# Retention units ahead of the first layer, and a table of powers that goes through memory, in a kernel of retention and two MLPs

## The chip, the cores and the metric

The kernel runs on one core of a Trainium2 chip. The metric is the time of one execution on the device in microseconds (us). The engines are TensorE (PE in the rows, PEld for its weight loads), VectorE (DVE), ScalarE (ACT), GpSimd (POOL) and SyncE (SP), which here issues every DMA.

## What is computed

Retention over 2 batches, 8 heads, 768 positions of 64 features; its output, 1536 tokens of 512 features, goes through two MLPs of width 2048 one after the other.

```
for b in range(nb):                       # blocks of the sequence
    intra = einsum('bhic,bhjc->bhij', qb, kb) * Dmask      # Dmask: lam ** (i - j), below the diagonal
    intra = einsum('bhij,bhjd->bhid', intra, vb)
    inter = einsum('bhid,bhde->bhie', qb * lam_pow, kv_state)
    out[:, :, sl] = intra + inter
    kv_state = lam_block * kv_state + einsum('bhsd,bhse->bhde', kb * rev_pow, vb)
x = out.transpose(0, 2, 1, 3).reshape(1536, 512)
x = square(relu(x @ w_in)) @ w_out        # first MLP (l = 0)
h = x @ w_in2;  out = maximum(0.01 * h, h) @ w_out2        # second MLP (l = 1)
```

The MLP weights arrive as 8-byte floats, which no engine computes with. They are split on the chip into two 4-byte parts, and every product of the MLPs is made of three matmuls: high by high, high by low, low by high.

## The kernel before

**Retention.** There are 12 units, one for each batch and each 128 positions (chunk). For a unit i, `load` fetches k, q and v (256 KB each); `transposes(i)` turns k and q on PE and copies them out on ACT (kT, qT); `scale_q` makes qS on DVE for chunks after the first; `scores(i)` fills two PSUM banks; `mask(i)` multiplies them on DVE with the table of powers DTr into Pm; `state(i)` scales k with kdec on POOL (kd), multiplies it with v on PE, and updates st on DVE with the help of tmp from POOL; `output(i)` is made of matmuls with st and qS (not in the first chunk of a batch) and with Pm and v, and `split` writes its high part on ACT (xhi) and its low part on DVE (xlo). Four units fill a token tile of 512 columns, so there are three token tiles. The last chunk of a batch needs no `state`.

**The table.** On DVE `pw` gets 8 rows of powers, one row for each head in a partition of its own. `table()` spreads them: for each head one DMA of 64 KB, in which every one of the 128 partitions of DTr reads 512 bytes of that row, shifted by one element. `kdec`, which `state` needs, is copied on DVE out of DTr, and LR comes from `rows_of_powers` on PE.

**The MLPs.** `steps` lists l, s, t: two MLPs, four stages of 512 of the 2048 columns, three token tiles; 24 in all. `first` has four groups of 12 matmuls 128x512, each group evacuated as g (high and low part ghi, glo); `second` has four groups of 12, added up in `acc`. So a `first` or a `second` is 48 matmuls, and the MLPs are 24 x 96 = 2304 (the last group is cut into halves of 256 columns). A stage needs four blocks of weights, two of w_in and two of w_out, 1 MB each. `fetch` issues the DMA of a block into one of two buffers `raw`, and `convert` turns it into high and low parts with seven DVE instructions (L104 to L114) and two on ACT.

**The order.** Within `retention` the order on SP and PE is that of the program; on the other engines, and after retention everywhere, a scheduler orders the instructions. PE starts an instruction only after the one ahead of it in its order. The loop over the units fetches a block in every second unit, calls `convert` in every second unit from the fourth on, and from the fifth unit on puts one group of `meanwhile`, the first and second layer of the first step, behind each unit. After the loop the rest of `meanwhile` follows, and then `first` of a step and `second` of the one before it take turns. `warm` is a number of transposes whose results are not used.

Of the kernel before, what the change touches and what calls it, by code (L numbers as in the profile page):

```python
# [19 lines left out]
def tile_retention_then_two_mlps(  # L20
# [28 lines left out]
    ctx.enter_context(nc.allow_non_contiguous_dma(reason="head slices, power table"))  # L49
    xp = ctx.enter_context(tc.tile_pool(name="xp", bufs=1))  # L50
# [41 lines left out]
    def convert():  # L92
        if not fetched:
            return
# [9 lines left out]
        ve.tensor_scalar(out=hf, in0=hf, scalar1=2.0 ** -15, scalar2=122368.0, op0=ALU.max, op1=ALU.min)  # L104
        ve.tensor_scalar(out=hb, in0=hb, scalar1=3, scalar2=0x3FFFFFFF,
                         op0=ALU.logical_shift_left, op1=ALU.bitwise_and)
        ve.scalar_tensor_tensor(out=hb, in0=w_hi, scalar=0xC0000000, in1=hb,  # L107
                                op0=ALU.bitwise_and, op1=ALU.bitwise_or)

        ve.tensor_scalar(out=rb, in0=hb, scalar1=0xFF800000, scalar2=None, op0=ALU.bitwise_and)  # L110
        ve.scalar_tensor_tensor(out=rf, in0=w_lo, scalar=2.0 ** -52, in1=rf, op0=ALU.mult, op1=ALU.mult)
        ve.tensor_tensor(out=hf, in0=hf, in1=rf, op=ALU.add)  # L112
        nc.scalar.copy(hi, hf)  # L113
        ve.tensor_tensor(out=lo, in0=hf, in1=hi, op=ALU.subtract)  # L114
# [13 lines left out]
    def retention(ctx_att, att, meanwhile):  # L128
# [83 lines left out]
        kdec = att.tile([P, NP, 2], F32, name="kdec")  # L212

        def table():

            for h in range(H):
                row = pw[h:h + 1, 1:C + 1]
                dma(DTr[:, h % 2, h // 2, :],
                    bass.AP(tensor=row.tensor, offset=row.offset, ap=[list(row.ap[0]), [1, P], [1, C]]))

        def rows_of_powers():
            ps = bank().rearrange("p (a s) -> p a s", a=NP)
            for p in range(NP):
                nc.tensor.matmul(ps[:, p, :], mine[:, p * P:(p + 1) * P], pw[:, 0:C][:, ::-1], start=True, stop=True)
            return ps

        def transposes(i):
            for name, dst in (("k", kT), ("q", qT)):
# [4 lines left out]
                if i == 0:  # L233
                    warm(3 if name == "k" else 8)
# [26 lines left out]
        def state(n):  # L261
            b, c = units[n]
            if c == NCH - 1:
# [5 lines left out]
                in1=kdec.rearrange("s a (r o) -> s a r o", o=1).to_broadcast([P, NP, 2, D]), op=ALU.mult)  # L269
# [37 lines left out]
        FILL = TT // C  # L307
        table()
        load(0, "v")
        load(2, "kq")  # L310
# [120 lines left out]
    for _ in second(*steps[-1]):  # L431
        pass
# [25 lines left out]
```

## Time and profile before

| | us |
|---|---|
| median of 3 runs | 618.4 (618.04 to 618.56) |
| the profiled execution | 618.69 |
| its span, from the first to the last instruction | 616.9 |
| PE busy | 587.6 |
| DVE busy | 402.0 |
| ACT busy | 250.9 |
| POOL busy | 25.0 |

The span is what the trace shows; 1.8 us of the execution lie around it. The chain of work that ended last is 88% PE, 5% DVE and 3% DMA, so the time is read along PE: how long it works for the MLPs, and what keeps it from doing so. The windows of the trace give busy time, the clock that TensorE was granted (1.00 is 2.4 GHz, 0.50 is 1.2 GHz) and the share of the 16 DMA engines for any stretch.

### The profile page before, as it was taken

How to read it: one execution, taken by the hardware profiler on the slowest of the kernel's cores; microseconds unless marked ns; L12 is line 12 of the kernel's file. 1: busy time of each engine (PE TensorE's matmuls, PEld its weight loads, DVE VectorE, ACT ScalarE, POOL GpSimd, SP SyncE). 2: the span in 40 equal slices, each digit the busy share in tenths (PEclk: the TensorE clock that was granted, in tenths of full speed). 3: DMA queues.
4: the chain of work that ended last, by engine and by line, in shares of the span. 5: the costliest groups of instructions: out<-in, count | busy, mean ns of one | idle time of the engine just before them, and what ended most of it. 6: DMA issues, size and time to landing. Idle time of an engine off the chain costs nothing.

```text
span 616.9 us, 7702 instructions
## 1 busy us (share of the span) xinstructions
PE 587.6 (95%) x3162; PEld 489.5 (79%) x3162; DVE 402.0 (65%) x545; ACT 250.9 (41%) x378; POOL 25.0 (4%) x37
## 2 busy tenths in 40 slices
PE   7088899999999999999999999999999999999997
PEld 6077688888888888888888888888888888888886
DVE  2169999999592939475776977582959453343342
ACT  2034364586654437244636353534333141132120
POOL 1133130000000000000000000000000000000000
PEclk9599799999999999999999999999999999999999
DMA  6799842434421221204040403040210000000112
GB/s 81 84 228 268 212 122 70 163 109 140 133 72 65 70 69 68 69 4 134 0 137 0 127 10 133 5 137 0 69 69 0 1 0 2 0 2 0 69 41 96
DMA packets 57411, 47.16 MB, mean 76 GB/s; under 512 B 38304, under 2 KB 39584, under 8 KB 57376
## 3 DMA queue, kind: packets, MB, share of 16 engines
q1 hardware_dynamic: 57376, 46.67, 27.0%
q8 instruction: 25, 0.41, 0.3%
q14 instruction: 10, 0.08, 0.0%
HBM read 42.99 MB, written 3.15 MB: 75 GB/s over the span
## 4 chain that ended last, share of the span: by engine, by line
PE 88%; DVE 5%; DMA 3%; SPq 2%; ACT 1%; issue 1%; DVEq 0%
PE ps L397 42%; PE ps L362 14%; PE ps L363 14%; PE ps L364 14%; SPq L61 2%; DMA DTr<-pw 2%; DMA raw<-in_moe_w_in 1%; DVE Pm L254 1%; PE ps L249 1%; PE ps L298 1%; PE ps L300 1%; PE ps L273 1%; PE ps L232 0%; DVE hb L107 0%; DVE hb L112 0%
## 5 line engine op out<-in xcount | busy, mean ns | idle before, releaser
L362 PE MATMUL ps<-xhi,whi 128*128 128x512 f32 x384 | 150.8, 393 | 0.0
L363 PE MATMUL ps<-xlo,whi 128*128 128x512 f32 x384 | 150.1, 391 | 0.0
L364 PE MATMUL ps<-xhi,wlo 128*128 128x512 f32 x384 | 150.1, 391 | 0.0
L402 DVE TENSOR_TENSOR acc<-ps,acc 128x512 f32<-128x512 f32 (+1 forms) x73 | 49.7, 681 | 65.0 <-PE ps L397 64.9
L362 PEld LDWEIGHTS ps<-xhi,whi 128*128 128x128 f32 x384 | 72.6, 189 | 15.6 <-issue 0.2
L364 PEld LDWEIGHTS ps<-xhi,wlo 128*128 128x128 f32 x384 | 72.5, 189 | 15.3
L363 PEld LDWEIGHTS ps<-xlo,whi 128*128 128x128 f32 x384 | 72.7, 189 | 15.0
L397 PE MATMUL ps<-wlo,ghi 128*128 128x512 f32 (+1 forms) x196 | 75.4, 385 | 0.0
L397 PE MATMUL ps<-whi,glo 128*128 128x512 f32 (+1 forms) x196 | 75.4, 385 | 0.0
L397 PE MATMUL ps<-whi,ghi 128*128 128x512 f32 (+1 forms) x196 | 75.4, 385 | 0.0
L397 PE MATMUL ps<-ghi,whi 128*128 128x512 f32 x192 | 75.0, 391 | 0.0
L397 PE MATMUL ps<-glo,whi 128*128 128x512 f32 x192 | 74.7, 389 | 0.0
L397 PE MATMUL ps<-ghi,wlo 128*128 128x512 f32 x192 | 74.7, 389 | 0.0
L372 ACT ACTIVATE r<-ps 128x512 f32<-128x512 f32 x48 | 28.7, 598 | 93.0 <-PE ps L364 92.8
L367 ACT ACTIVATE r<-ps 128x512 f32<-128x512 f32 x48 | 28.5, 593 | 64.8 <-PE ps L364 64.8
L373 DVE TENSOR_TENSOR r<-ps,r 128x512 f32<-128x512 f32 x48 | 33.1, 689 | 33.0 <-ACT r L372 33.0
L114 DVE TENSOR_TENSOR wlo<-hb,whi 128x1024 fp32r<-128x1024 f32 x32 | 40.3, 1271 | 21.8 <-ACT whi L113 21.8
L370 DVE TENSOR_TENSOR glo<-r,ghi 128x512 fp32r<-128x512 f32 x48 | 33.4, 698 | 31.9 <-ACT r L369 31.8
L113 ACT CAST whi<-hb 128x1024 fp32r<-128x1024 f32 x32 | 33.1, 1051 | 42.1 <-PE ps L397 29.3
L65 DVE TENSOR_TENSOR glo<-r,ghi 128x512 fp32r<-128x512 f32 x48 | 33.2, 691 | 22.2 <-ACT ghi L64 22.0
L64 ACT CAST ghi<-r 128x512 fp32r<-128x512 f32 x48 | 29.8, 620 | 37.5 <-DVE r L373 37.5
L103 ACT ACTIVATE hb<-raw 128x1024 f32<-128x1024 f32 x32 | 36.7, 1148 | 16.2 <-DMA raw<-in_moe_w_out 6.2
(70 smaller groups left out, 725.5 us busy)
## 6 DMA issues: line engine op xcount, KB each, us to landing
raw<-in_moe_w_in SPq DMA_DIRECT2D x16, 1024.0 KB, 5.4
raw<-in_moe_w_out SPq DMA_DIRECT2D x16, 1024.0 KB, 5.0
k<-in_k SPq DMA_DIRECT2D x12, 256.0 KB, 5.8
q<-in_q SPq DMA_DIRECT2D x12, 256.0 KB, 4.8
v<-in_v SPq DMA_DIRECT2D x12, 256.0 KB, 6.4
out<-acc SPq DMA_DIRECT2D x11, 256.0 KB, 2.0
DTr<-pw SPq DMA_DIRECT2D x8, 64.0 KB, 9.9
out<-acc SPq DMA_DIRECT2D x2, 128.0 KB, 1.7
```

The costliest lines, as they stand in the source:

```text
L64: nc.scalar.copy(hi, src)
L65: nc.vector.tensor_tensor(out=lo, in0=src, in1=hi, op=ALU.subtract)
L103: nc.scalar.activation(hf, w_hi.bitcast(F32), AF.Abs)
L113: nc.scalar.copy(hi, hf)
L114: ve.tensor_tensor(out=lo, in0=hf, in1=hi, op=ALU.subtract)
L362: nc.tensor.matmul(ps, hi_w[:, kk, ms], xhi[t][:, kk], start=kk == 0, stop=False)
L363: nc.tensor.matmul(ps, hi_w[:, kk, ms], xlo[t][:, kk], start=False, stop=False)
L364: nc.tensor.matmul(ps, lo_w[:, kk, ms], xhi[t][:, kk], start=False, stop=kk == KD - 1)
L370: nc.vector.tensor_tensor(out=glo[:, m], in0=r, in1=ghi[:, m], op=ALU.subtract)
L373: nc.vector.tensor_tensor(out=r, in0=ps, in1=r, op=ALU.max)
L397: nc.tensor.matmul(ps, a, b, start=kk == 0 and n == 0, stop=kk == KF - 1 and n == 2)
L402: nc.vector.tensor_tensor(out=a, in0=ps, in1=a, op=ALU.add)
```

## The change

Four things are different, and one follows from them.

- The table: `pw` is stored to memory (`tab`, 8 KB), and two DMAs of 256 KB read it back, one for even heads and one for odd ones, with 512 bytes for each partition and head. The store is ahead of three loads on SP, the two reads behind two of them. `kdec` comes from a transpose of `pw` on PE and a copy on ACT.
- The start: `state(0)` and the transposes of k of unit 2 stand ahead of `mask(0)`, and `output(0)`, the transposes of q of unit 2, `mask(1)` and `scores(2)` stand ahead of the loop; there are fewer `warm`.
- The loop: no group of the MLPs is in it. Only units 0 and 2 fetch a block. `convert` became a generator, so that one unit makes one of the seven DVE instructions of a block (units 5 and 10 make two), 12 in all; these are held in the order of the program.
- The MLPs: for stage 0 of the first MLP the three `first` come in a row, then the `second` of tiles 2, 0 and 1. Tile 2 keeps its g in the space of acc0 and acc1 until its `second` is done. After that `first` and `second` take turns as before. The weights of the following stage are asked for at every sixth piece of that list.
- The rest of `fetch` and `convert` of stage 0 follows behind retention, beside the first layer.

```diff
-    def retention(ctx_att, att, meanwhile):
+    def retention(ctx_att, att):
...
-        kdec = att.tile([P, NP, 2], F32, name="kdec")
+        kdec = att.tile([P, H], F32, name="kdec")
+
+        tab = dram.tile([H, W], F32, name="tab")
 
         def table():
-
-            for h in range(H):
-                row = pw[h:h + 1, 1:C + 1]
-                dma(DTr[:, h % 2, h // 2, :],
-                    bass.AP(tensor=row.tensor, offset=row.offset, ap=[list(row.ap[0]), [1, P], [1, C]]))
+            for par in range(2):
+                row = tab[par:par + 1, 1:C + 1]
+                dma(DTr[:, par], bass.AP(tensor=row.tensor, offset=row.offset, ap=[[1, P], [2 * W, NP], [1, C]]))
+
+        def column_of_powers():
+            ps = bank()[:, 0:H]
+            nc.tensor.transpose(ps, pw[:, 1:C + 1], ident[0:H, 0:H])
+            nc.scalar.copy(kdec, ps)
...
         n_units = len(units)
         FILL = TT // C
+        dma(tab, pw)
+        load(0, "v")
+        load(2, "k")
         table()
-        load(0, "v")
-        load(2, "kq")
+        load(2, "q")
         load(1, "v")
         transposes(0)
         scores(0)
-        lr_psum = rows_of_powers()
-        nc.scalar.copy(LR, lr_psum)
+        column_of_powers()
+        rows_of_powers()
         scale_q(1, transposes(1))
         scores(1)
-        for par in range(2):
-            ve.tensor_copy(kdec[:, :, par], DT[:, par, :, C - 1])
+        state(0)
+        transposes(2, "k")
         mask(0)
-        warm(6)
+        warm(2)
+        output(0)
+        scale_q(2, transposes(2, "q"))
+        mask(1)
+        scores(2)
         for i in range(n_units):
-            if 0 < i < n_units - 2:
-                scale_q(i + 2, transposes(i + 2))
+            if i:
+                if i + 2 < n_units:
+                    scale_q(i + 2, transposes(i + 2))
             if i + 3 < n_units:
                 load(i + 3, "kq")
             if i + 2 < n_units:
                 load(i + 2, "v")
-            if i % 2 == 0:
+            if i in (0, 2):
                 fetch()
-            state(i)
-            output(i)
-            if i == 0:
-                warm(6)
-                scale_q(2, transposes(2))
-            if i + 1 < n_units:
-                mask(i + 1)
-            if i + 2 < n_units:
-                scores(i + 2)
-            if i >= FILL - 1 and i % 2:
-                convert()
-            if i >= FILL:
-                next(meanwhile, None)
-        for _ in meanwhile:
-            pass
+            if i:
+                state(i)
+                output(i)
+                if i + 1 < n_units:
+                    mask(i + 1)
+                if i + 2 < n_units:
+                    scores(i + 2)
+            if i > 1:
+                convert(2 if i % 5 == 0 else 1)
...
     def first(l, s, t):
         hi_w, lo_w = wts[l, s][:2]
-        n = steps.index((l, s, t)) % 2
-        ghi = place[n].tile([P, KF, TT], F32R, tag=f"ghi{n}", name=f"ghi{n}")
-        glo = place[n].tile([P, KF, TT], F32R, tag=f"glo{n}", name=f"glo{n}")
+
+        n = steps.index((l, s, t)) % 2 if l or s else t
+        tags = (f"ghi{n}", f"glo{n}") if n < 2 else ("acc0", "acc1")
+        ghi, glo = (place[n % 2].tile([P, KF, TT], F32R, tag=tag, name=tag) for tag in tags)
...
-            retention(ctx_att, att, chain(first(*steps[0]), second(*steps[0])))
+            retention(ctx_att, att)
     place[1] = ctx.enter_context(tc.tile_pool(name="late", bufs=1, reuse_waits="tile"))
+    line = [first(*steps[0]), first(*steps[1]), first(*steps[2])]
+    line += [second(*steps[2]), second(*steps[0]), second(*steps[1]), first(*steps[3])]
+    for i in range(4, len(steps)):
+        line += [first(*steps[i]), second(*steps[i - 1])]
+    line.append(second(*steps[-1]))
     turn = 0
-    for i, (l, s, t) in enumerate(steps):
-        if t == 0:
-            ls = l * NS + s + 1
-            if ls < 2 * NS:
-                load_w(*divmod(ls, NS))
-        work = first(l, s, t) if i else ()
-        if i > 1:
-            work = chain(work, second(*steps[i - 1]))
+    for i, work in enumerate(line):
+        if i % (2 * NTILE) == 0 and i // (2 * NTILE) + 1 < 2 * NS:
+            load_w(*divmod(i // (2 * NTILE) + 1, NS))
         for _ in work:
             turn += 1
-            if turn % 4 == 1:
+            if turn % 4 == 1 or turn == 2:
                 fetch()
-            elif turn % 4 == 3:
-                convert()
-    for _ in second(*steps[-1]):
-        pass
+            if turn % 4 == 3 or turn == 1:
+                convert(pin=turn < 8)
```

What this does to the order on three engines stands below. A row is an instruction in its place, with what it writes and reads; the line numbers of the changed kernel are higher.

On SP at the start of the program, before: the eight DMAs of the table stand behind the loads of units 0 and 1.

```order
L61 DMA q<-in_q 128x8x64
L61 DMA DTr<-pw 128x1x128 x8
L61 DMA v<-in_v 128x8x64
L61 DMA k<-in_k 128x8x64
L61 DMA q<-in_q 128x8x64
L61 DMA v<-in_v 128x8x64
```

The same place on SP, now:

```order
L62 DMA q<-in_q 128x8x64
L62 DMA tab<-pw 8x256
L62 DMA v<-in_v 128x8x64
L62 DMA k<-in_k 128x8x64
L62 DMA DTr<-tab 128x4x128 x2
L62 DMA q<-in_q 128x8x64
L62 DMA v<-in_v 128x8x64
```

One store and two reads took the place of eight DMAs, and v of unit 0 and k of unit 2 moved ahead of the reads.

On PE in the middle of retention, before, at unit 6: L362 to L364 are the end of a group of the first layer, L232 the transposes, L273 `state`, L300 `output`, L249 `scores`, and then the next group begins.

```order
L362 MATMUL ps<-xhi_297,whi_73 128x512
L363 MATMUL ps<-xlo_298,whi_73 128x512
L364 MATMUL ps<-xhi_297,wlo_74 128x512
L232 MATMUL ps<-ident,k 128x128 x4
L232 MATMUL ps<-ident,q 128x128 x4
L273 MATMUL ps<-v,kd 64x64 x8
L300 MATMUL ps<-Pm,v 64x128 x8
L249 MATMUL ps<-qT,kT 128x128 x8
L362 MATMUL ps<-xhi_297,whi_73 128x512
```

On PE, now, at the one place where retention and first layer meet: the end of `output(11)` (L324, L326) and the first matmuls of the MLPs (L390 to L392).

```order
L324 MATMUL ps<-qS,st_174 64x128 x2
L326 MATMUL ps<-Pm,v 64x128 x2
L324 MATMUL ps<-qS,st_174 64x128 x2
L326 MATMUL ps<-Pm,v 64x128 x2
L390 MATMUL ps<-xhi_287,whi_75 128x512
L391 MATMUL ps<-xlo_288,whi_75 128x512
L392 MATMUL ps<-xhi_287,wlo_76 128x512
```

The groups of 12 that stood between the units moved behind the last unit.

On DVE in retention, before, around units 3 to 5: L104 to L114 are the instructions of a conversion, L254 is `mask`, L242 qS, L285 the update of st, L65 xlo.

```order
L110 TENSOR_SCALAR rb<-hb 128x1024
L65 TENSOR_TENSOR xlo_298<-ps,xhi_297 128x4x128
L254 TENSOR_TENSOR Pm<-ps,DTr 128x512 x2
L111 SCALAR_TENSOR_TENSOR rb<-raw,rb 128x1024
L242 TENSOR_TENSOR qS<-ps,LR 128x512
L285 TENSOR_TENSOR st_169<-ps,tmp 64x4x64 x2
L112 TENSOR_TENSOR hb<-hb,rb 128x1024
L65 TENSOR_TENSOR xlo_298<-ps,xhi_297 128x4x128
L254 TENSOR_TENSOR Pm<-ps,DTr 128x512 x2
L114 TENSOR_TENSOR wlo_74<-hb,whi_73 128x4x256
L104 TENSOR_SCALAR hb<-hb 128x1024
L105 TENSOR_SCALAR hb<-hb 128x1024
```

The same stretch on DVE, now (L280 is `mask`, L268 qS, L311 st, L66 xlo):

```order
L280 TENSOR_TENSOR Pm<-ps,DTr 128x512 x2
L104 TENSOR_SCALAR hb<-hb 128x1024
L268 TENSOR_TENSOR qS<-ps,LR 128x512
L311 TENSOR_TENSOR st_174<-ps,tmp 64x4x64 x2
L66 TENSOR_TENSOR xlo_288<-ps,xhi_287 128x4x128
L280 TENSOR_TENSOR Pm<-ps,DTr 128x512 x2
L105 TENSOR_SCALAR hb<-hb 128x1024
```

Between two masks stands one instruction of a conversion, where there were two to three.

## Rows read from the trace of the kernel before

**Rows 1.** The page's first line, then rows of the timeline of PE and of the chain that ended last (start us, us, what): the first second-layer matmul behind the last retention unit, one whole `second`, the last matmul.

```profile
span 616.9 us, 7702 instructions
...
106.93 0.50 PE L397 MATMUL ps<-ghi,whi 128*128 128x512 f32 x1
...
156.18 10.88 PE ps L397 x48
...
613.01 0.28 PE L397 MATMUL ps<-whi,glo 128*128 128x256 f32 x1
```

**Rows 2.** Windows of the trace: from and to in us, length, then busy us (and instructions) of PE, PEld, DVE, ACT and POOL, granted clock of PE, mean share of the 16 DMA engines, GB/s that they moved.

```profile
12.00:14.00 2.00, 1.27 (x16) 0.91 (x12) 0.00 (x0) 0.00 (x0) 0.00 (x0) 1.00 0.66 25
...
30.00:40.00 10.00, 9.28 (x122) 8.25 (x120) 6.12 (x12) 2.74 (x5) 4.64 (x7) 0.86 1.01 244
40.00:50.00 10.00, 8.62 (x140) 7.48 (x136) 8.29 (x13) 4.43 (x7) 2.84 (x4) 1.00 0.95 242
50.00:60.00 10.00, 7.36 (x101) 6.03 (x100) 9.81 (x15) 5.39 (x8) 4.19 (x4) 1.00 0.98 249
60.00:70.00 10.00, 8.36 (x98) 7.11 (x98) 9.93 (x12) 3.85 (x6) 1.04 (x1) 1.00 0.93 217
...
70.00:75.00 5.00, 4.15 (x21) 3.54 (x22) 4.87 (x9) 1.80 (x4) 0.45 (x1) 0.54 1.09 266
```

**Rows 3.** The timeline of all engines at the start (start us, us, engine, line, operation, and in brackets how long the engine was idle before it and what it waited for): the table's DMAs, PE's last work before the wait, the copy for kdec, the first mask.

```profile
6.54 14.16 SPq L61 DMA_DIRECT2D DTr<-pw  x8
...
12.39 0.87 PE L164 MATMUL ps<-ident 128*128 128x128 f32 x6
...
26.96 0.17 DVE L319 COPY kdec<-DTr 128x4 f32<-128x4 f32 x1 [20.51 <-DMA DTr<-pw]
...
28.19 1.28 DVE L254 TENSOR_TENSOR Pm<-ps,DTr 128x512 f32<-128x512 f32 x2
```

**Rows 4.** The chain that ended last, at its start: the load of lam, and the last piece of pw.

```profile
0.74 1.36 DMA sq<-in_lam
...
6.21 0.25 DVE pw L184
```

**Rows 5.** DMA issues by line: the two half-width stores of the result, with their count, KB of each, and median us from issue to landing.

```profile
out<-acc SPq DMA_DIRECT2D x2, 128.0 KB, 1.7
```

**Rows 6.** The timeline again: `scores` of unit 1, and the first transposes of a unit in the loop, for units 3, 4 and 7.

```profile
11.30 1.16 PE L249 MATMUL ps<-qT,kT 64*128 64x128 f32 x16 [0.73 <-ACT qT L236]
...
36.07 0.66 PE L232 MATMUL ps<-ident,k 128*128 128x128 f32 x4
...
41.60 0.63 PE L232 MATMUL ps<-ident,k 128*128 128x128 f32 x4 [0.99 <-DMA k<-in_k]
...
57.37 0.66 PE L232 MATMUL ps<-ident,k 128*128 128x128 f32 x4
```

**Rows 7.** The timeline of PE: `output` of unit 6, the first chunk of its batch; and one unit where PE never paused: its transposes, `state`, the first matmuls of `output`, `scores`, and what follows them.

```profile
67.31 1.05 PE L300 MATMUL ps<-Pm,v 128*64 128x128 f32 x16
...
85.05 0.60 PE L232 MATMUL ps<-ident,k 128*128 128x128 f32 x4
...
86.02 0.69 PE L273 MATMUL ps<-v,kd 128*64 128x64 f32 x16
86.53 0.39 PE L298 MATMUL ps<-qS,st 128*64 128x128 f32 x4
...
88.38 1.16 PE L249 MATMUL ps<-qT,kT 64*128 64x128 f32 x16
89.47 0.50 PE L362 MATMUL ps<-xhi,whi 128*128 128x512 f32 x1
```

**Rows 8.** The timeline of DVE in retention: qS, st, a conversion's instruction, xlo, mask, and two more of the conversion.

```profile
46.06 0.68 DVE L242 TENSOR_TENSOR qS<-ps,LR 128x512 f32<-128x512 f32 x1
...
46.66 0.86 DVE L285 TENSOR_TENSOR st<-ps,tmp 64x256 f32<-64x256 f32 x2
...
47.55 0.75 DVE L110 TENSOR_SCALAR rb<-hb 128x1024 uint32<-128x1024 uint32 x1
...
48.34 0.69 DVE L65 TENSOR_TENSOR xlo<-ps,xhi 128x512 fp32r<-128x512 f32 x1
...
48.95 1.28 DVE L254 TENSOR_TENSOR Pm<-ps,DTr 128x512 f32<-128x512 f32 x2
50.14 1.21 DVE L111 SCALAR_TENSOR_TENSOR rb<-raw,rb 128x1024 f32<-128x1024 uint32 x1
...
55.89 1.93 DVE L114 TENSOR_TENSOR wlo<-hb,whi 128x1024 fp32r<-128x1024 f32 x1
```

**Rows 9.** The timeline of PE around a pause: `scores` of unit 8 after it, and the matmul that follows.

```profile
70.85 2.08 PE L249 MATMUL ps<-qT,kT 64*128 64x128 f32 x16 [2.49 <-ACT qT L236]
72.86 0.79 PE L362 MATMUL ps<-xhi,whi 128*128 128x512 f32 x1
```

**Rows 10.** The timeline of ACT in the first layer: the first of the three instructions that evacuate a group, the same of the next group, and the two instructions of a conversion.

```profile
127.46 0.59 ACT L367 ACTIVATE r<-ps 128x512 f32<-128x512 f32 x1
...
129.29 0.58 ACT L367 ACTIVATE r<-ps 128x512 f32<-128x512 f32 x1
...
131.80 1.06 ACT L113 CAST whi<-hb 128x1024 fp32r<-128x1024 f32 x1 [0.60 <-DVE hb L112]
...
135.90 1.15 ACT L103 ACTIVATE hb<-raw 128x1024 f32<-128x1024 f32 x1 [1.22 <-DVE glo L370]
```

More of the change, by code (lines that the diff above doesn't have):

```diff
@@ L49, in tile_retention_then_two_mlps @@
     ctx.enter_context(nc.allow_non_contiguous_dma(reason="head slices, power table"))
+    dram = ctx.enter_context(tc.tile_pool(name="dram", bufs=1, space=bass.MemoryType.DRAM))
     xp = ctx.enter_context(tc.tile_pool(name="xp", bufs=1))
@@ L90, in fetch, with converting @@
             fetched.append((r, hi, lo))
-    def convert():
-        if not fetched:
-            return
+    def converting():
         r, hi, lo = fetched.pop(0)
@@ L103, in convert @@
         nc.scalar.activation(hf, w_hi.bitcast(F32), AF.Abs)
[L104 to L112, printed above, removed]
-        nc.scalar.copy(hi, hf)
-        ve.tensor_tensor(out=lo, in0=hf, in1=hi, op=ALU.subtract)
+        yield ve.tensor_scalar(out=hf, in0=hf, scalar1=2.0 ** -15, scalar2=122368.0, op0=ALU.max, op1=ALU.min)
+        yield ve.tensor_scalar(out=hb, in0=hb, scalar1=3, scalar2=0x3FFFFFFF,
+                               op0=ALU.logical_shift_left, op1=ALU.bitwise_and)
+        yield ve.scalar_tensor_tensor(out=hb, in0=w_hi, scalar=0xC0000000, in1=hb,
+                                      op0=ALU.bitwise_and, op1=ALU.bitwise_or)
+        yield ve.tensor_scalar(out=rb, in0=hb, scalar1=0xFF800000, scalar2=None, op0=ALU.bitwise_and)
+        yield ve.scalar_tensor_tensor(out=rf, in0=w_lo, scalar=2.0 ** -52, in1=rf, op0=ALU.mult, op1=ALU.mult)
+        yield ve.tensor_tensor(out=hf, in0=hf, in1=rf, op=ALU.add)
+        nc.scalar.copy(hi, hf)
+        yield ve.tensor_tensor(out=lo, in0=hf, in1=hi, op=ALU.subtract)
+    at_work = []
+    def convert(steps=None, pin=True):
+        done = 0
+        while steps is None or done < steps:
+            if not at_work:
+                if not fetched or (steps is None and done):
+                    return
+                at_work.append(converting())
+            step = next(at_work[0], None)
+            if step is None:
+                at_work.pop()
+                if steps is None:
+                    return
+            else:
+                done += 1
+                if pin:
+                    tc.keep_in_program_order(step)
     wts, todo, fetched = {}, [], []
@@ L224, in rows_of_powers, with transposes @@
                 nc.tensor.matmul(ps[:, p, :], mine[:, p * P:(p + 1) * P], pw[:, 0:C][:, ::-1], start=True, stop=True)
-            return ps
-        def transposes(i):
-            for name, dst in (("k", kT), ("q", qT)):
+            nc.scalar.copy(LR, ps)
+        def transposes(i, names="kq"):
+            for name in names:
+                dst = {"k": kT, "q": qT}[name]
                 ps = bank().rearrange("p (a s) -> p a s", a=NP)
@@ L233, in transposes @@
                 if i == 0:
-                    warm(3 if name == "k" else 8)
+                    warm(3 if name == "k" else 4)
                 dst[i] = tr.tile([P, NP, C], F32, tag=name, name=name + "T")
@@ L268, in state @@
                 out=kd, in0=kn.rearrange("s (a r) d -> s a r d", r=2),
-                in1=kdec.rearrange("s a (r o) -> s a r o", o=1).to_broadcast([P, NP, 2, D]), op=ALU.mult)
+                in1=kdec.rearrange("s (a r o) -> s a r o", r=2, o=1).to_broadcast([P, NP, 2, D]), op=ALU.mult)
             ps = bank()[:, 0:NP * D].rearrange("p (a e) -> p a e", a=NP)
```

## The prediction

> **What bounds the kernel now.** I read the end first. Behind the last retention unit PE works for the MLPs without a pause from 106.93 us to 613.01 + 0.28 = 613.3 us [rows 1]. One `first` or `second` of 48 matmuls takes 10.88 us there, 0.2267 us a matmul. At 106.93 us 72 of the 2304 matmuls were done (the `first` of step 0 and half of its `second`), so the MLPs need 506.4 + 72 x 0.2267 = 522.7 us of PE, and 613.3 - 522.7 = 90.6 us of PE time went to something else. I call that the lead. Nothing in the change touches the 522.7 us or the 3.6 us from 613.3 to the end of the span, so the question is how long the lead becomes.
>
> The start comes second. The last piece of pw is ready at 6.46 us [rows 4], the first mask starts at 28.19 us [rows 3]. In between DVE waits 20.51 us for the table's DMAs; PE has its last work at 12.39 us and waits as well. While the table moves, the DMA engines carry 25 GB/s; with the loads of k, q, v and weights they carry 217 to 249 [rows 2].
>
> Then the stretch from the first mask to the end of retention. From 50 to 70 us DVE is busy 9.8 to 9.9 us of 10 and PE 7.4 to 8.4 [rows 2]: DVE bounds it, since it converts weights between the units. From 30 to 60 us the DMA engines are full as well (0.95 to 1.01).
>
> **The change part by part.** I build the new lead piece by piece: it ends when PE has done `output(11)`, since the MLPs then follow without other work between.
>
> *The table.* The eight DMAs took from 6.54 to about 28 us, 21.5 us for 524 KB [rows 3]. Their source is one partition per head. The new ones: a store of 8 KB, which I put at 2.0 us from issue to landing, between the 1.36 us of the load of lam [rows 4] and the 1.7 us of the 128 KB stores with an issue ahead of it [rows 5]. So the reads start at 8.5 us. Ahead of them in the queue are v0 and k2, from about 7.0 us on; at 238 GB/s (the mean of the four windows [rows 2]) v0, k2 and table, 1.05 MB, are through at 11.4 us, and I add 1 us for landing: first mask at **12.5 us**. No row shows a DMA that reads the same 4 KB of memory 128 times. From below the queue bounds it at 10.7 us (8.5 us and 2.2 us for 524 KB at 238 GB/s), from above the old table, 8.5 + 21.5 = 30 us. I take the near end, because the loads of k read memory in 256-byte pieces, smaller than the 512 here, and share the 238 GB/s; but they read different addresses, and the far end stays as a rival.
>
> The trace shows the slow table with a source in SBUF. A rule of the Trainium skill speaks against the new source: the page "SBUF — State Buffer", section "A bandwidth-pool intuition that's wrong", gives memory 32 ports of about 22.5 GB/s each. If the whole 8 KB lay behind one of them, 524 KB would take an estimated 23 us, the first mask would come at about 32 us, and the time would be some 614 us; no run here shows which it is. Told by rows, this is the first rival below.
>
> *The start.* `scores(1)` starts at 11.30 us and ends about 1.1 us later [rows 6]; fewer warms change nothing, since the copies of kT and qT set that time. kdec no longer waits for the table, so `state(0)` and the k transposes run before the mask. After the mask come on the chain: 1.28 us of mask [rows 3], `output(0)` 1.05, q transposes 0.5, the copy 0.6, `scores(2)` 1.1, and some 0.5 for the handovers: 5 us. The loop starts at **17.5 us**; before it was 36.07 us, 7.9 us behind the mask [rows 6].
>
> *The units on PE.* A unit without pauses: transposes 0.97, `state` 0.51, `output` 1.85, `scores` 1.09, together 4.42 us from start to start [rows 7]. Unit 5 has no `state` (3.91), unit 6 is a first chunk (3.62, its `output` takes 1.05).
>
> *The loads.* Up to q of unit 6, SP issues in this order from 7.0 us on: v0, k2, table, q2, v1, three loads of unit 3's turn, a block, three, three, a block, k6 and q6, 6.55 MB. At 238 GB/s that is 27.5 us, so q6 lands at **34.5 us**. PE alone would be there at 17.5 + 3 x 4.42 = 30.8 us, so the loads set this point; at 217 and 249 GB/s [rows 2] it is 37.2 and 33.3 us. Behind it a unit needs 786 KB, 3.3 us, less than PE needs. Only two blocks of weights are in the way, where six were.
>
> *From there to the end of retention on PE.* 4.42 + 3.91 + 3.62 + 3 x 4.42 + 2.36 (unit 10, nothing to load) + 1.85 (unit 11) = 29.4 us.
>
> *DVE in that stretch.* By start-to-start times [rows 8] a unit costs qS 0.60, st 0.89, xlo 0.61, mask 1.19, so 3.29 us; five units and six conversion instructions of 0.7 to 1.9 us (6.6 us) are 23 us. DVE no longer bounds it. I add 1.5 us for handovers. **The lead: 34.5 + 29.4 + 1.5 = 65.4 us**, against 90.6.
>
> *What was taken out comes back beside the first layer.* In the 32.6 us of the three `first`, DVE has the rest of the second block (4 us), three blocks of about 7 us and 12 glo, as long as an xlo, 0.6: 32 us. ACT has 12 evacuations of 1.83 us (from one to the next [rows 10]) and eight conversion instructions of 1.1: 30.8 us. Both are nearly full, and neither has to be on time, except at one place: the `second` of tile 2 starts right behind its `first` and needs the last g after nine matmuls, 2.0 us. ACT's three instructions alone take 1.83 us, a conversion's instruction between them 1.06. The new order on PE puts eight matmuls of the next group ahead of the two that need the last glo. I price it at **0.5 us**, between 0 and 4 (all of a late block). Weights are not late there: w_out is needed 32.6 us behind retention instead of 10.9. For later stages the list asks for weights 20 groups ahead instead of 24; 20 groups are 54 us for four blocks of 7 us of DVE, which costs nothing.
>
> **Sum:** 618.7 - (90.6 - 65.4) + 0.5 = **594.0 us** by the profiled execution. That lies 0.3 us above the median of the three runs, so against the median it is 593.7; I leave 594.0.
>
> **The rivals.**
>
> *The table is as slow out of memory as out of SBUF.* First mask at 30 us, loads queue behind it as before, q6 at 30 + 5.5 MB / 238 GB/s = 53 us, lead 84 us: 612.5 us. For it: all reads go to 4 KB. Against it: nothing in the trace but the rate of other loads.
>
> *The other side: the reads of those 4 KB run one after another, slower still.* Each us of table then shifts q6 by one. The lead reaches the old one (less the 0.5 us) when the table lands at 36.4 us, in 28 us, 18.8 GB/s; below that the kernel becomes slower. At half of the old pace, 43 us, it would be 634 us. Against it: 18.8 GB/s is less than the old table reached [rows 2].
>
> *PE is throttled or held up in the units.* Behind a pause of 2.49 us the granted clock fell to the lower level: `scores` took 2.08 us instead of 1.16, and 70 to 75 us shows 0.54 [rows 2, 9]. Such a fall cost about 3 us. The waits for loads at units 4 and 6 are 1 to 2.5 us, and no MLP group stands between units. Against it: from 40 to 60 us PE was busy only 7.4 to 8.6 of 10, with a pause of 0.99 us among others, and the clock stayed at 1.00 [rows 2, 6]. Two falls, or units of 5.3 us as from 41.60 to 57.37 us, three units [rows 6], add 3 to 6 us: 597 to 600.5 us.
>
> *The MLPs don't run densely at first.* If the `second` of tile 2 waits for ACT and DVE with all the work put off, 4 us, and stage 1's weights then lag by a block, 7 us more: 598 to 605 us.
>
> *The change does nothing* would need the 20.51 us wait and the DVE bound to come back elsewhere in just that size.
>
> **How the numbers follow.** Forecast (588.5 to 597): 0.68. Throttle or long units (597 to 601): 0.14. First layers not dense (598 to 605): 0.05. Table at the old pace (about 612.5): 0.07. Slower table: 0.05. No change: 0.01. The range 588.5 to 604 goes from loads that are never late and no handovers (lead 30.8 + 29.4 = 60.2, 588.3 us) to the two middle rivals, and leaves out some 0.17. A measurement here can tell about 0.2% from no change, 1.2 us: faster 0.94, same 0.01, slower 0.05.
>
> **What would show it.** Right: the first mask starts at 11 to 14 us; `output(11)` ends at 61 to 69 us; between the units PE waits for q loads up to unit 6 and hardly behind it; granted clock 1.00 from 17 us on; `second` of tile 2 waits under 1 us; from there 10.88 us per 48 matmuls. Wrong: a first mask at 20 us or later (the table), DVE at 9.8 of 10 in retention (the bound stayed), clock near 0.5 in a window of the units, or PE pauses in the first layers.

## The result and the profile after

The kernel after takes 594.8 us, the median of three executions from 594.7 to 595.5; a fourth, a slow one of 2083.87 us, is left out. The kernel before took 618.5 us on the same chip. The ratio is 0.962, 95% interval 0.960 to 0.964; by the medians it is 23.6 us less. The profiled execution took 594.66 us.

First the page's first line, rows of PE's timeline (the first matmul of the first layer, the last matmul of the program), and one of the chain that ended last (start us, us, what). They answer to [rows 1].

```profile
span 592.8 us, 7681 instructions
...
65.26 0.50 PE L390 MATMUL ps<-xhi,whi 128*128 128x512 f32 x1
...
153.93 10.88 PE ps L425 x48
...
589.00 0.28 PE L425 MATMUL ps<-whi,glo 128*128 128x256 f32 x1
```

A second layer is still 10.88 us. The last matmul ends at 589.28 us; less the 522.7 us of the MLPs that leaves a lead of 66.6 us, against 90.6. At 65.26 us all retention is done, so 1.3 us of the lead are lost behind it.

The timeline and the chain at the start, against [rows 3, 4]: SP's issue of the store and of the two reads, the reads in the chain, the two halves of the first mask, what PE does behind it, and the first transposes of the loop.

```profile
6.56 0.30 SPq L62 DMA_DIRECT2D tab<-pw  x1
...
6.56 1.50 DMA tab<-pw
8.12 0.66 SPq L62
8.82 5.07 DMA DTr<-tab
...
13.09 0.69 DVE L280 TENSOR_TENSOR Pm<-ps,DTr 128x512 f32<-128x512 f32 x1 [6.62 <-DMA DTr<-tab]
...
13.98 0.69 DVE L280 TENSOR_TENSOR Pm<-ps,DTr 128x512 f32<-128x512 f32 x1 [0.21 <-DMA DTr<-tab]
...
14.73 0.66 PE L258 MATMUL ps<-ident,k 128*128 128x128 f32 x4 [0.17 <-DVE Pm L280]
...
15.54 1.09 PE L326 MATMUL ps<-Pm,v 128*64 128x128 f32 x16
...
18.98 0.66 PE L258 MATMUL ps<-ident,k 128*128 128x128 f32 x4
```

Each of the two reads takes some 5.1 us to landing; from the issue of the first (8.12 us) to the landing of the second (8.82 + 5.07 = 13.89 us) it is 5.8 us, where the eight DMAs took 21.5. The first mask stands at 13.09 us instead of 28.19.

Windows of the trace (columns as in rows 2):

```profile
12.00:14.00 2.00, 1.29 (x20) 1.13 (x22) 0.71 (x2) 0.00 (x0) 0.00 (x0) 1.00 1.14 265
30.00:40.00 10.00, 8.95 (x144) 7.78 (x143) 7.79 (x13) 4.56 (x7) 3.32 (x4) 1.00 1.08 260
40.00:50.00 10.00, 10.00 (x156) 8.91 (x156) 9.76 (x17) 5.34 (x9) 3.80 (x4) 1.00 1.14 213
50.00:60.00 10.00, 10.00 (x164) 8.91 (x162) 9.84 (x18) 3.45 (x7) 4.79 (x6) 1.00 0.83 194
...
35.80:65.30 29.50, 29.50 (x477) 26.45 (x477) 27.38 (x45) 12.45 (x21) 11.00 (x13) 1.00 0.85 180
```

From 12 to 14 us the DMA engines carry 265 GB/s, with the table among it, where they carried 25 [rows 2]. From 40 us on PE is busy all the time, at a granted clock of 1.00; but so, nearly, is DVE. PE's waits (what for, us in total, times, longest us) are few:

```profile
PE ps L258 <- DMA k<-in_k: 1.6, 2, 0.8
...
PE ps L258 <- DMA q<-in_q: 0.9, 2, 0.6
...
PE ps L425 <- ACT acc L396: 0.3, 1, 0.3
PE ps L425 <- DVE acc L398: 0.2, 1, 0.2
```

The first two are the loads at units 4 and 6, as forecast. The last two are the `second` of tile 2, whose activations lie in acc0 and acc1.

### The profile page after: what moved, and what is told of

Its sections match the earlier page's. It is cut to its first block, busy times and chain, and to the rows that moved or that the text cites. A ratio compares the mean times of both kernels' runs of the same rounds, so it can differ in the third digit from the quotient of the medians.

```text
span 592.8 us, 7681 instructions
## 1 busy us (share of the span) xinstructions
PE 582.5 (98%) x3149; PEld 485.1 (82%) x3149; DVE 399.2 (67%) x543; ACT 253.3 (43%) x379; POOL 24.4 (4%) x37
## 4 chain that ended last, share of the span: by engine, by line
PE 90%; DMA 5%; DVE 3%; ACT 1%; issue 0%; SPq 0%; ACTq 0%; DVEq 0%
PE ps L425 44%; PE ps L390 13%; PE ps L392 13%; PE ps L391 13%; DMA q<-in_q 2%; PE ps L326 1%; PE ps L324 1%; PE ps L275 1%; PE ps L258 1%; DMA raw<-in_moe_w_in 1%; DMA DTr<-tab 1%; PE ps L299 1%; DVE rb L111 1%; DVE hb L112 0%; DVE hb L107 0%; DVE glo L398 0%
## 5 line engine op out<-in xcount | busy, mean ns | idle before, releaser
L390 PE MATMUL ps<-xhi,whi 128*128 128x512 f32 x384 | 149.5, 389 | 0.0
L392 PE MATMUL ps<-xhi,wlo 128*128 128x512 f32 x384 | 149.3, 389 | 0.0
L392 PEld LDWEIGHTS ps<-xhi,wlo 128*128 128x128 f32 x384 | 72.1, 188 | 15.2 <-DVE wlo L114 0.3
L390 PEld LDWEIGHTS ps<-xhi,whi 128*128 128x128 f32 x384 | 72.1, 188 | 15.1 <-issue 0.2
L425 PE MATMUL ps<-ghi,whi 128*128 128x512 f32 x176 | 68.5, 389 | 0.0
L425 PE MATMUL ps<-glo,whi 128*128 128x512 f32 x176 | 68.5, 389 | 0.0
L425 PE MATMUL ps<-ghi,wlo 128*128 128x512 f32 x176 | 68.5, 389 | 0.0
L400 ACT ACTIVATE r<-ps 128x512 f32<-128x512 f32 x48 | 28.7, 599 | 93.0 <-PE ps L392 92.6
L398 DVE TENSOR_TENSOR glo<-r,ghi 128x512 fp32r<-128x512 f32 x44 | 30.3, 689 | 31.6 <-ACT r L397 31.4
L114 DVE TENSOR_TENSOR wlo<-hb,whi 128x1024 fp32r<-128x1024 f32 x32 | 38.7, 1222 | 18.3 <-ACT whi L113 18.2
L113 ACT CAST whi<-hb 128x1024 fp32r<-128x1024 f32 x32 | 33.1, 1050 | 38.0 <-PE ps L425 27.4
L66 DVE TENSOR_TENSOR glo<-r,ghi 128x512 fp32r<-128x512 f32 x48 | 33.2, 691 | 22.2 <-ACT ghi L65 22.0
L65 ACT CAST ghi<-r 128x512 fp32r<-128x512 f32 x48 | 29.8, 620 | 37.5 <-DVE r L401 37.5
L425 PEld LDWEIGHTS ps<-whi,ghi 128*128 128x128 f32 x196 | 36.8, 188 | 7.4
```

The source lines that it names most:

```text
L65: nc.scalar.copy(hi, src)
L66: nc.vector.tensor_tensor(out=lo, in0=src, in1=hi, op=ALU.subtract)
L114: yield ve.tensor_tensor(out=lo, in0=hf, in1=hi, op=ALU.subtract)
L390: nc.tensor.matmul(ps, hi_w[:, kk, ms], xhi[t][:, kk], start=kk == 0, stop=False)
L392: nc.tensor.matmul(ps, lo_w[:, kk, ms], xhi[t][:, kk], start=False, stop=kk == KD - 1)
L398: nc.vector.tensor_tensor(out=glo[:, m], in0=r, in1=ghi[:, m], op=ALU.subtract)
```

## The experiments

My theory is the prediction's: the table's wait is the larger part and passes to the end us for us; the rest comes because PE, no longer DVE, sets the units once most conversions have left the loop. The rivals give each part another cause. "Lead" is the end of the last matmul less 522.7 us, from each profiled execution; times are medians.

| kernel | us | ratio to before, 95% | lead, us |
|---|---|---|---|
| after | 594.8 | 0.960 to 0.964 | 66.6 |
| after, again (c0) | 595.5 | 0.962 to 0.964 | 66.5 |
| after, old table (e1) | 610.1 | 0.984 to 0.988 | 82.2 |
| before, new table (e2) | 602.2 | 0.971 to 0.975 | 72.4 |
| table in eight reads (e3) | 598.0 | 0.964 to 0.970 | 70.6 |
| thick conversions (e4) | 610.1 | 0.984 to 0.989 | 81.2 |
| second block late (e5) | 595.4 | 0.962 to 0.967 | 71.4 |
| usual layer order (e6) | 598.1 | 0.966 to 0.969 | 68.7 |
| tile 0's second first (e7, e11) | 593.9, 593.7 | 0.959 to 0.962, 0.959 to 0.961 | 65.3 (e7) |
| both blocks late (e8) | 594.3 | 0.959 to 0.962 | 66.7 |
| first layers in halves (e9) | 592.8 | 0.957 to 0.961 | 64.2 |
| halves, block at unit 9 (e10) | 592.9 | 0.958 to 0.961 | 64.6 |

**The table alone, and all but the table (e1, e2).** e1 is the kernel after with

```diff
-            for par in range(2):
-                row = tab[par:par + 1, 1:C + 1]
-                dma(DTr[:, par], bass.AP(..., ap=[[1, P], [2 * W, NP], [1, C]]))
+            for h in range(H):
+                row = pw[h:h + 1, 1:C + 1]
+                dma(DTr[:, h % 2, h // 2, :], bass.AP(..., ap=[list(row.ap[0]), [1, P], [1, C]]))
...
-        dma(tab, pw)
```

> The kernel after, with the eight table transfers of the kernel before put back (read straight from pw, one a head, no store to memory). My theory, as the prediction has it: the first mask waits for the table again, at 26 to 29 us where the kernel after has 13.1; the loop of units starts its transposes about 6 us behind it (18.98 against 13.09 in the kernel after), at 33 to 35; loads have arrived by then, so no transposes wait for k or q (the 2.4 us of such waits at units 4 and 6 go), three units of about 4.42 us follow and then the 29.4 us to the last output; the lead comes to 76 to 78 us instead of 65.3 and the time to 606.5 us (604 to 611). Rival: the loads are what sets the units, and the wait for the table was hidden behind them; then the end moves by less than 4 us and the time is under 599.

e2 makes the opposite edit in the kernel before, with `dma(tab, pw)`, v of unit 0 and k of unit 2 ahead of the reads and q of unit 2 behind them.

> The kernel before with one change only: the table of powers is stored to memory and read back by two transfers, as in the kernel after; the order of units, weights blocks and layers is as before. My theory: the first mask comes at 13 to 15 us where it came at 28.2, and the end comes earlier by most of these 15 us, less what the loads and a VectorE that still converts whole blocks between units take back: 605 us (602 to 610). Rival: the gain of the change is in its order of work, and what the table gives is lost to units that wait for VectorE and loads; then the time is over 612.

e1 came to 610.1 us: 15 us more, within my bounds and 3.6 above my value. Its first mask starts at 28.29 us, 15.20 later than in the kernel after, and its first layer at 80.50, 15.24 later. SP's timeline, those two rows, a window and two of PE's waits of e1:

```profile
6.85 14.93 SPq L62 DMA_DIRECT2D DTr<-pw  x8
21.88 2.82 SPq L62 DMA_DIRECT2D q<-in_q  x1
...
27.70 0.96 SPq L62 DMA_DIRECT2D k<-in_k  x1
...
28.29 1.29 DVE L281 TENSOR_TENSOR Pm<-ps,DTr 128x512 f32<-128x512 f32 x2 [21.84 <-DMA DTr<-pw]
...
80.50 0.50 PE L390 MATMUL ps<-xhi,whi 128*128 128x512 f32 x1
...
20.00:30.00 10.00, 0.92 (x16) 0.95 (x16) 1.71 (x3) 0.00 (x0) 0.00 (x0) 0.50 0.68 72
...
PE ps L259 <- DVE Pm L281: 0.9, 1, 0.9
...
PE ps L259 <- DMA q<-in_q: 0.3, 1, 0.3
```

The eight transfers hold SP's queue for 14.93 us, and every later load is issued behind them: k of unit 3 at 27.70 us instead of 12.23, and from 20 to 30 us the DMA engines carry 72 GB/s. So loads had not all "arrived by then", as I had written: unit 6 still begins late, with 0.3 us of waiting for q and 0.9 that the profile puts down to a mask. The equal shift of mask and first layer is also no proof that nothing was hidden, since two things cancel. Behind its wait of 16.6 us PE works at a granted clock of 0.50, and the loop starts 7.4 us behind the mask (at 35.71 us) where the kernel after has 5.9. The three units from there to q of unit 6 take 15.3 us where it has 16.8. The rival, an end that moves by less than 4 us, falls.

e2 came to 602.2 us, 16.4 less than before and at the low end of my range; its first mask starts at 13.08 us. The table alone is worth 16.4 us and the order alone 8.5; together they gave 23.6, 1.3 less than their sum, which is no more than the spread of e2's runs. In e2 DVE is busy 9.8 of 10 us from 30 to 50 us, as before from 50 to 70 [rows 2].

**Place or number of the table's reads (e3).**

```diff
-            for par in range(2):
-                row = tab[par:par + 1, 1:C + 1]
-                dma(DTr[:, par], bass.AP(..., ap=[[1, P], [2 * W, NP], [1, C]]))
+            for h in range(H):
+                row = tab[h:h + 1, 1:C + 1]
+                dma(DTr[:, h % 2, h // 2, :], bass.AP(..., ap=[[1, P], [1, C]]))
```

> The kernel after, with the table read from its copy in memory by eight transfers of one head each instead of two of four heads. My theory: it is the place that it is read from that counts, so the last of them lands at 16 to 19 us (eight issues of about 0.6 us from 8.1 us on, and 1.5 to 5 us behind the last), the later loads are issued 4 us later, and the time is 597.5 us (595 to 600). Rival: the number of transfers made the table slow; then the first mask stands at 24 us or later and the time is over 603.

598.0 us. DMA issues of the kernels after, e3 and e1, one row each (count, KB each, median us to landing), then SP and the first mask of e3:

```profile
DTr<-tab SPq DMA_DIRECT2D x2, 256.0 KB, 5.1
```
```profile
DTr<-tab SPq DMA_DIRECT2D x8, 64.0 KB, 3.3
...
7.98 4.19 SPq L62 DMA_DIRECT2D DTr<-tab  x8
...
16.14 0.69 DVE L280 TENSOR_TENSOR Pm<-ps,DTr 128x512 f32<-128x512 f32 x1 [9.69 <-DMA DTr<-tab]
```
```profile
DTr<-pw SPq DMA_DIRECT2D x8, 64.0 KB, 10.0
```

Eight transfers out of memory hold SP for 4.19 us, eight out of SBUF for 14.93. The place is worth 12.1 of the 15.2 us of the first mask (28.29 to 16.14), the smaller number the other 3.1. "Place" takes two things together: memory instead of SBUF, and one block of 8 KB instead of one partition for each head. No run separates them.

**Units first, but conversions as before (e4).**

```diff
-            if i in (0, 2):
+            if i % 2 == 0:
                 fetch()
...
-            if i > 1:
-                convert(2 if i % 5 == 0 else 1)
+            if i >= FILL - 1 and i % 2:
+                convert()
```

> The kernel after, but with weights blocks fetched at every second unit and converted whole behind units 3, 5, 7 and 9, as the kernel before spaces them: four blocks in the loop of units instead of 12 steps (1.7 blocks). A block is 6.9 us of VectorE (0.68 + 0.68 + 1.22 + 0.68 + 1.22 + 1.22 + 1.22 from the kernel after), a unit without one 3.6 us. My theory: VectorE is level with TensorE in the units of the kernel after (9.8 of each 10 us), so nearly all of the 16 us added to it goes onto the path; the lead is 76 to 80 us instead of 65.3, the first layers and the first second layer lose less than the 1.5 us that they lost; 607 us (603 to 610). Rival: TensorE sets the units and VectorE's full rows are only work pulled ahead; then the time is under 599.

610.1 us, 15 more than the kernel after. Two windows, and PE's waits from 20 to 80 us, of e4:

```profile
50.00:60.00 10.00, 7.75 (x80) 6.31 (x78) 9.88 (x15) 4.10 (x6) 5.30 (x5) 0.83 0.83 202
60.00:70.00 10.00, 7.61 (x116) 6.71 (x116) 9.90 (x14) 3.33 (x6) 2.27 (x3) 0.93 0.78 197
...
PE ps L324 <- DVE st L311: 4.3, 3, 2.4
PE ps L258 <- DMA k<-in_k: 2.3, 3, 0.9
PE ps L324 <- DVE qS L268: 1.9, 1, 1.9
```

The time is just above my range (603 to 610), and so is the lead, 81.2 us against 76 to 80. DVE is full, PE waits for it, and the granted clock falls to 0.83 and 0.93 in these windows. So the order by itself is no gain: with the new table, the old order with thick conversions (e2, 602.2 us) beats the new order with thick ones by 8 us. That this is so because the old one has MLP matmuls between units for PE is my reading; no run isolates it. With the new table, retention first pays only together with conversions taken out of the loop. Two more fetches also stand in the loop here; PE's waits for k and q are 4.0 us here (1.7 of them q), 1.5 more than in the kernel after and far less than the 15.

**The second block's fetch (e5).** `if i in (0, 2)` becomes `if i in (0, 5)`.

> The kernel after once more, unchanged, so that the next three have it on their own chip: 595.2 us (594.6 to 595.8).

> The kernel after, with the second weights block (1 MB) fetched at unit 5 instead of unit 2, behind the loads of k and q for units 5 to 8; the conversion steps are where they were (this block's first step comes behind unit 8). My theory: the loads ahead of q set when unit 6 begins, so the waits of 0.78 and 0.27 us there go and the time is 594.2 us (593.6 to 594.9). Rival: VectorE, level with TensorE from 40 us on, takes the gain back: 595.2 us as before.

The control gave 595.5 us. e5 gave 595.4, from 594.0 to 599.5, above my range, and settles little. No wait is left at unit 6, but e6 below, which loads as the kernel after does, has none there either: in the profiled executions of both, PE waited 1.27 and 0.6 us for k and q of unit 4, the granted clock fell, and from q of unit 4 to k of unit 5 it took 5.6 us instead of 4.0, so that the loads of unit 6 were there in time. Unit 9, whose loads are now issued behind the block, waits 0.96 us for its q, and the profiled execution (599.5 us) lost more at the `second` of tile 2. The windows behind unit 4, in e5 and then in e6:

```profile
26.00:28.00 2.00, 1.86 (x22) 1.56 (x24) 1.90 (x4) 0.83 (x2) 0.00 (x0) 0.57 1.37 219
28.00:30.00 2.00, 2.00 (x26) 2.00 (x24) 1.27 (x3) 0.00 (x0) 1.61 (x2) 0.58 1.39 223
```
```profile
26.00:28.00 2.00, 1.97 (x24) 1.70 (x26) 2.00 (x4) 0.72 (x2) 0.01 (x1) 0.60 1.30 219
28.00:30.00 2.00, 2.00 (x24) 2.00 (x22) 0.98 (x3) 0.00 (x0) 1.93 (x3) 0.55 1.26 236
```

The row of e5 at the `second` of tile 2, and the windows around it:

```profile
103.50 0.50 PE L425 MATMUL ps<-acc,whi 128*128 128x512 f32 x1 [1.55 <-DVE acc L398]
...
100.00:105.00 5.00, 3.18 (x13) 2.05 (x12) 3.24 (x5) 3.88 (x6) 0.00 (x0) 0.98 0.66 215
105.00:110.00 5.00, 5.00 (x16) 4.02 (x16) 5.00 (x7) 2.29 (x4) 0.00 (x0) 0.68 0.00 0
```

That handover, 0.5 us of waits in the kernel after, is a fragile place, and it can cost a fall of the clock besides.

**The order of stage 0's layers (e6, e7).** e6 takes the loop's pattern from the start, with g of tile 2 in its usual place:

```diff
-    line = [first(*steps[0]), first(*steps[1]), first(*steps[2])]
-    line += [second(*steps[2]), second(*steps[0]), second(*steps[1]), first(*steps[3])]
-    for i in range(4, len(steps)):
+    line = [first(*steps[0])]
+    for i in range(1, len(steps)):
```

> The kernel after, with the layers of stage 0 in the usual order (first of tile 0, first of 1, second of 0, first of 2, second of 1, ...), so that nothing is lent. My theory: the second layer of tile 0 starts two first layers behind the units (65.3 + 21.8 = 87.1 us), and its third group of 12 matmuls needs the last w_out block at 92.5, which was ready only at 96.3 in the kernel after: a stall of 3 to 4 us, 599 us (597 to 600.5). Rival: with a first layer less ahead of it VectorE finishes the block sooner and no stall comes, nor the 1.1 us lost at the second layer of tile 2: 594.2 to 595.5 us.

e7:

```diff
-    line += [second(*steps[2]), second(*steps[0]), second(*steps[1]), first(*steps[3])]
+    line += [second(*steps[0]), second(*steps[2]), second(*steps[1]), first(*steps[3])]
...
-        tags = (f"ghi{n}", f"glo{n}") if n < 2 else ("acc0", "acc1")
+        tags = (f"ghi{n}", f"glo{n}") if n < 2 else ("whi11", "wlo11")
...
+        if i == 5:
+            load_w(0, 1, parts=(1,))
```

> The kernel after, with the second layers of stage 0 in the order of tiles 0, 2, 1 instead of 2, 0, 1. For that the squared activations of tile 2 lie in the place of the w_out weights of the next stage, whose two blocks are therefore fetched two slots later. My theory: the 1.1 us lost at the start of the second layer of tile 2 is the wait for its activations, finished last; with tile 0 first they have 8.6 us of cover: 594.1 us (593.4 to 594.8). Rival: the pauses come from VectorE and ScalarE being full from 90 to 110 us and stay, or come back at the later blocks: 595.2 us or more.

e6: 598.1 us, 2.5 more than the control beside it. The wait is where I put it, 2.1 us instead of 3 to 4: retention ended 0.8 us later here (66.07 us), behind the fall of the clock just shown, so the block was needed at 93.8 us and not 92.5, and its first half (whi) is all that the first matmul needs:

```profile
95.91 0.50 PE L425 MATMUL ps<-ghi,whi 128*128 128x512 f32 x1 [2.11 <-ACT whi L113]
```

So three first layers ahead give w_out time. Behind retention this execution loses 2.6 us (68.7 - 66.07) where the kernel after loses 1.3; the 0.8 us by which retention ended later are the clock's and not the order's, so the order is worth 1.3 us by the traces and at most the 2.5 of the medians. e7: 593.9 us, 1.7 less than the control, and 593.7 on another chip. PE has no wait behind retention, which ends at 65.10 us, and the lead falls to 65.3 us.

**More out of the way (e8 to e11).** e8 is e7 with fetches at units 2 and 5 and the 12 steps behind units 4 to 11:

```diff
-            if i in (0, 2):
+            if i in (2, 5):
...
-            if i > 1:
-                convert(2 if i % 5 == 0 else 1)
+            if i > 3:
+                convert(2 if i % 2 else 1)
```

> The kernel with tile 0's second layer first (593.85 us, 0.9606 of the kernel before), in which both weights blocks of the loop are fetched behind the loads of q for unit 6 (at units 2 and 5 instead of 0 and 2), and the same 12 conversion steps stand behind units 4 to 11 instead of 2 to 11. My theory: the loads ahead of q of unit 6 fall from 6.55 to 4.45 MB, so the waits for k and q at units 4 and 6 go (2.4 us by their own rows, at most 3.5 with what stands around them), and VectorE, level with TensorE in the last units already, gives back some: 592.9 us (591.5 to 594.0). Rival: VectorE sets the pace of the last eight units, which now hold 1.5 conversion steps each instead of 1.2 (0.3 x 8 x 1.0 = 2.4 us more, and more where steps come in front of a mask): 594.5 us or more.

e9 has `(2, 6)` and `convert(1)` in the same places, and

```diff
+    def firsts():
+        parts = [first(*steps[t]) for t in range(NTILE)]
+        for half in range(2):
+            for f in parts:
+                ...
+    line = [firsts(), (), ()]
```

> As the last, but with one conversion step a unit (8 in all) behind units 4 to 11, the second block fetched at unit 6, and the first layers of stage 0 in two halves: groups 0 and 1 of all three tiles, which need only the first block of w_in, then groups 2 and 3 of all three. The second block is thereby needed 16.3 us behind the last unit instead of 5.4, and most of its conversion leaves the loop of units. My theory: neither loads nor VectorE hold the units back any more, three units from 18.98 us take 13.3 us instead of 16.8, so the lead is 62 us instead of 65.3 and the time is 590.5 us (589.3 to 592.5). Rival: the three blocks to convert within the 32.6 us of the first layers (20.7 us, and 8.3 us for the activations) are too much, and w_out stalls the second layers: 593 us or more.

e8: 594.3 us, no gain over e7, above my range and just under the rival's 594.5. Its waits for loads did not go but moved, to unit 9, where the two blocks now stand ahead:

```profile
47.66 0.63 PE L257 MATMUL ps<-ident,k 128*128 128x128 f32 x4 [1.53 <-DMA k<-in_k]
48.76 0.63 PE L257 MATMUL ps<-ident,q 128*128 128x128 f32 x4 [0.46 <-DMA q<-in_q]
```

e9: 592.8 us against 590.5 expected, above my range (589.3 to 592.5). Its ratio is the lowest of all, 0.957 to 0.961, but the intervals of e7 to e11 overlap, so the times alone do not rank these kernels. Unit 6's q transposes start at 33.48 us instead of 35.77, but at unit 10 loads wait again (0.49 and 0.57 us). The last pair:

> As the last kernel (halves), with the second weights block fetched at unit 9, behind all loads of k and q, and only the first block converted in the loop, one step behind each of units 5 to 11. My theory: the waits for k and q at unit 10 (0.49 and 0.57 us) were for the 1 MB fetched at unit 6, and go; the second block lands at about 60 us and is converted within the 16.3 us of the first halves: 591.7 us (590.8 to 592.6). Rival: from 40 us on VectorE sets the pace (its own rows of a unit add to 3.6 us, and 4.8 with a step of 1.22), and the wait for loads only stands where the wait for VectorE would; then nothing changes: 592.5 to 593.5 us.

> The kernel with tile 0's second layer first once more, unchanged, on the chip of the last: 593.85 us (593.4 to 594.3). It tells what of the difference between the two lies in the kernels.

e10: 592.9 us; e11: 593.7. The time is the rival's, but neither theory is right about e10. PE runs without a wait from 20 to 60 us, unit 11 starts at 53.51 us (56.37 in the kernel after), so VectorE does not set the pace there. Of the gain 2.0 us come back in the first layers, as waits for a block's conversion, the first block's at 62.69 us and the second's at 80.92. The rows between them are the first step of the second block on ACT, the first glo, and the first step of that block on DVE:

```profile
53.51 0.66 PE L257 MATMUL ps<-ident,k 128*128 128x128 f32 x4
...
62.69 0.50 PE L389 MATMUL ps<-xhi,whi 128*128 128x512 f32 x1 [0.38 <-ACT whi L112]
...
65.36 1.12 ACT L102 ACTIVATE hb<-raw 128x1024 f32<-128x1024 f32 x1 [2.23 <-DVE wlo L113]
...
69.97 0.69 DVE L397 TENSOR_TENSOR glo<-r,ghi 128x512 fp32r<-128x512 f32 x1 [4.99 <-ACT r L396]
...
72.84 0.69 DVE L103 TENSOR_SCALAR hb<-hb 128x1024 f32<-128x1024 f32 x1
...
80.92 0.50 PE L389 MATMUL ps<-xhi,whi 128*128 128x512 f32 x1 [1.62 <-ACT whi L112]
```

The 1.62 us are not the price of a full DVE. In its order the block's first step stands behind two glo, so it is idle for 4.99 us, 3.5 of them with ACT's step on the block done (66.48 us), and starts on the block at 72.84 us, where e9 starts at 65.89. Whether another order on DVE saves these 1.62 us was not tried. e10's loads with the steps of e9 (one unit earlier) might keep some of the 2 us too; that was not tried either.

## Why the prediction was right

**The table.** First mask 12.5 us forecast, 13.09 and 13.98 measured for its halves; the store took 1.50 us (2.0 put). The near end of the bounds was the right one: 128 partitions reading the same 8 KB travel at the rate of other loads (256 KB in 5.1 us, where a load of k, q or v of the same size takes 4.7 to 5.1, the medians of this run). By the Trainium skill's port rule ("SBUF — State Buffer", § "A bandwidth-pool intuition that's wrong") the estimate was 23 us; the measured 5.8 us for both reads speak against one port as the limit, and e3, with the same bytes, agrees. e1 and e2 make this part 15 to 16.4 us. The forecast's 15.7 us (28.19 to 12.5) stands.

**The start and the loads.** The loop starts at 18.98 us (17.5 forecast). Of the 1.5 us, 0.6 are the first mask, 0.3 its second half, which does not follow at once, and 0.8 the transposes of k of unit 2 with the two `warm`: I had them ahead of the mask, and PE starts them only behind it, at 14.73; 0.2 of the handovers was not needed. The miss cost nothing, because the loads set unit 6, as forecast. e7, with the same loads, shows it: its loop starts 1.7 us later still, and unit 6 does not (its k of unit 3 and its q of unit 6):

```profile
20.70 0.66 PE L257 MATMUL ps<-ident,k 128*128 128x128 f32 x4
...
35.61 0.63 PE L257 MATMUL ps<-ident,q 128*128 128x128 f32 x4 [0.42 <-DMA q<-in_q]
```

Unit 6's q is transposed at 35.77 us (34.5), behind waits for k and q at units 4 and 6, where forecast. The sum of MB over GB/s hit the point, but it hid a condition that e1 shows: the loads start early only because SP is free of the table. "Only two blocks of weights are in the way, where six were" was misread: the same two blocks stood ahead of q of unit 6 before (issued at 33.60 and 44.17 us), and four in that whole loop. The sum does not use it.

**PE from there on.** 29.4 us forecast, 65.26 - 35.77 = 29.5 measured; the 1.5 us for handovers were not needed and, by luck, made up for the 1.3 us by which unit 6 was late.

**DVE in that stretch** was mis-sized: 23 us put, 27.4 busy in 29.5. I counted five units and six conversion instructions; six masks, seven xlo and eight conversion instructions stand there. The margin was 2 us, not 6, and e4 shows the price when it is gone. "DVE at 9.8 of 10 in retention" was also my sign that the bound had stayed, and it showed: 9.76 and 9.84 from 40 to 60 us. The sign was badly chosen, since PE is busy 10.00 of 10 in the same windows and so sets the pace; waits of PE for DVE, as e4 has them, would have been the sign.

**The first layers.** 0.5 us put, within 0 to 4. Between 65.26 and the start of the second layer at 98.30 lie 33.04 us for 144 matmuls (32.6), 0.4 lost, and the `second` of tile 2 loses 1.1, since it takes 11.94 us instead of 10.88:

```profile
98.30 0.62 PE L425 MATMUL ps<-acc,whi 128*128 128x512 f32 x2
...
110.24 0.39 PE L425 MATMUL ps<-ghi,whi 128*128 128x512 f32 x1
```

Together that is 1.5 us (1.3 by the lead), most of it at the place named. e7 takes it away. The load on the engines was put too high: in these 33.04 us DVE is busy 28.7 us (32 forecast) and ACT 25.7 (30.8).

**Sum:** 594.0 forecast, 594.66 for the profiled execution. Lead 66.6 against 65.4 + 0.5: unit 6 late by 1.3 us, 0.1 more for the units, 0.8 more behind retention, and 1.5 of handovers not needed. The mechanism came out as told where it matters: the loads set unit 6, PE the units behind it, and the handover of tile 2 is where the first layers lose. That the lead came within 0.7 us is in part luck.

**The rivals.** The table's two rivals fall with the 5.07 us; the throttle, for the profiled execution, with a clock of 1.00 in all windows shown. It is no empty rival, though: e5 and e6 show the fall behind the waits at unit 4 that it named, at 1.6 us each (about 3 put). Of the kernel after itself, the profiled execution has a mean clock of 1.00 and the two others 0.996 and 0.997, as e6 has. Layers that don't run densely are e6, with 2.6 us lost behind retention, had stage 0 kept its usual order.

## What to carry to other kernels

Where a serial start gates everything, look at what its transfers read from and how long they hold the issuing queue: a bounce of 8 KB through memory (1.5 us) replaced a read that held it for 15 us. Moving work of one engine out of a stretch gains until another is level with it; then the order of the work and what that engine is given must be changed together, as e4 shows. What leaves a stretch has to find its place in the next: follow the last wait after each step, as from e7 to e10, where of 3 us gained in the units 2 came back as waits for weights.

## What the runs showed of the hardware

A read of 512 KB out of 8 KB of memory, by all partitions, in two transfers: 5.1 us to landing each and 5.8 us for both, beside other loads, 265 GB/s in all; the same bytes in eight transfers land in 3.3 us each (median) but hold SP for 4.19 us; out of eight partitions of SBUF 10.0 us each, and SP for 14.93. The clock does not follow the length of one pause alone: after 1.55 us at 103.50 in e5 the next 5 us show 0.68, while 2.11 us in e6 and 1.62 us in e10 left windows of 1.00, and a pause of 2.49 us cost a fall before [rows 2, 9]. Waits of 1.27 and 0.6 us at unit 4, 1.2 us apart, were followed by 0.55 to 0.60 for 4 us in e5 and e6; 1.50 and 0.58 us at the same unit in e11 left 1.00.
